# Transformer block with Strassen-type products: both bfloat16 products first in each gate/up unit, and another order for the first token pair of the down projection

## The chip, the cores and the metric

The kernel runs on one core of one Trainium2 chip. The metric is device time in microseconds, the median of several runs. The engines of the core are called PE (TensorE: matmuls and, beside them, weight loads), DVE (VectorE), ACT (ScalarE), POOL (GpSimd) and SP (SyncE, which issues nearly all DMAs here). Each engine works through its own instructions in order and waits on semaphores for the others.

## The reference

Inputs are bfloat16. `x` is 2048 tokens by 1024; the gate, up and down weights are 1024x3584, 1024x3584 and 3584x1024.

```python
mod = (silu(c) @ w_mod).reshape(1, 6, 1, -1)      # sa, ca, ga, sb, cb, gb
h = layernorm(x) * (1 + ca) + sa
x = x + ga * linear_attention(h, wqkv, wo)
h = layernorm(x) * (1 + cb) + sb
x = x + gb * ((gelu(h @ w_gate) * (h @ w_up)) @ w_down)
```

The change lies in the last line, in its gate/up products and its down projection, and in the second layernorm's modulation that feeds it.

## The kernel before, in words

**One level of Strassen-Winograd.** The gate/up products are done in 28 units, `unit(v)`, v = 0 to 27: two passes over halves of 1024 tokens (units 0 to 13 and 14 to 27), each pass over 14 slices of 256 columns of the weights. A unit computes, for gate (t = 0) and up (t = 1), a 2x2 block product with seven products instead of eight. A product is four matmuls of 128x128 weights against 512 tokens for each t, eight in all. P1 and P2 use the raw bfloat16 blocks; P3, P4, P5, P6 and P7 use sums and differences of blocks, held as float32r. The sums of the token side (`s_sum`, tiles ss, and a copy ar) are made once per pass; those of the weight side (`t_sum`, L1438, tiles tp, index k = 0, 1, 2, 4 on DVE with two instructions each, and k = 3 as two ACT copies, L1427) once per unit, ahead of it.

**Banks.** PSUM has eight banks, used as four pairs, one bank of each pair for t = 0 and one for t = 1: BA, BE, BB, BC. P1 goes to BA; ACT copies it to BB (`pcp`, L1470). P2 is accumulated onto BA, which then is one output block. P5 goes to BE and is copied to SBUF (`escp`, L1473). P6 is accumulated onto BB. DVE adds BB and the copy of P5 into BC (`padd`, L1476). P7 is accumulated onto BB, and DVE adds BB and the copy into BE (`padd` again). P3 is accumulated onto BC, P4 onto BB. Each of the four output blocks is then finished by a gelu of its gate bank (ACT, L1481) and a product with its up bank (DVE, `y_out`, L1485). The last of these, that of BB after P4, is *held*: it is issued in the next unit, between the two halves of P1. `y_store` writes two tiles per unit to DRAM.

**What sets the order.** From the gate/up units on, the order is the one in which the Python code emits instructions; no planner moves them (one does so for the attention part). PE runs the products in the order given to `unit`: 1, 5, 6, 2, 7, 3, 4; unit 0 has its own, `ORD0`, with 1, 2, 5, 6, two chunks of the attention's output projection, 7, 3, 4. P3 to P7 alternate t at each of the four steps; P1 and P2 run one t after the other. Extra work is put behind a product by `hook(v, k, fn)`: in units 1 to 8 the second layernorm of the later tokens on ACT, in units 5, 6, 9 and 10 its modulation (`mod2`, L754), in 10 to 14 the `s_sum`s (L1418) of the second pass, from 14 on the weight sums for the down projection (`b_sum`, L1577, 32 groups up to the end of unit 27). `wt_dma(v + 2)` reloads a weight slot behind P2.

**Down projection.** Eight token pairs j = 0 to 7 of 256 tokens. Its inner dimension is 14 blocks k; for k < `ns` it uses the same seven products (`dprod`, bfloat16 for 1 and 2, float32r for the others, one bank per product, banks of the pairs alternate with j), for the remaining k eight plain bfloat16 products (`plain`). `ns` is 13, but 6 for j = 0, since only six weight blocks have been summed by then; the rest (`lws`) is summed during pair 0. `y_load` fetches y into the tiles yl, `a_sum` (L1605, one ACT copy L1599) makes the token-side sums xs for the next pair, and `devac` (L1675, L1676) finishes one output quarter with two DVE instructions and a DMA. y of pair 1 overwrites that of pair 0 in the same tile.

The loop that places products and the work beside them in a unit:

Of the kernel before, what the change touches and what calls it, by code (L numbers as in the profile page):

```python
# [10 lines left out]
P = 128  # L11
# [4 lines left out]
CPG = NCH // NSG  # L16
SGW = P * CPG
NDC = D // P
# [328 lines left out]
def bass_adaLN_cond__linear_attn_block__geglu_ffn__prompt_kernel(  # L347
# [18 lines left out]
    with ExitStack() as es:  # L366
# [410 lines left out]
        def mod2(p, h, c0, n, dc0=0, dc1=NDC):  # L777
            mods(h2ap, r_h2p, (p, h), sc2, c0 * P, (c0 + n) * P, dc0, dc1, "h2")

        def mod2_act(h, c0=0, n=CPG, dc0=0, dc1=NDC):  # L780
            s0, s1 = c0 * P, (c0 + n) * P
            for dc in range(dc0, dc1):
                sA, sB, rs_ = sc2(dc)
                ap = h2ap((0, h), dc, s0, s1)
                sch.op(A, lambda e, ap=ap, sA=sA, sB=sB: e.activation(ap, ap, ACTF.Identity, bias=sB, scale=sA),
                       rd=r_h2(0, h, dc, dc + 1, s0, s1) + rs_, wr=r_h2(0, h, dc, dc + 1, s0, s1), note=f"h2modb {h}.{dc}")


        MC0 = 496
# [709 lines left out]
        def hook(v, k, fn):  # L1499
            HK.setdefault((v, k), []).append(fn)  # L1500

        def unit(v, order=(1, 5, 6, 2, 7, 3, 4)):
            more = v + 1 < 2 * NFP
            for k in order:
                if isinstance(k, tuple):
                    wo_chunk(*k)
                    continue
                if callable(k):
                    k()
                    continue  # L1510
                late = v == 0 and k == 2
                gb_, gk, yl, yh = (None, 1, 0, 0) if late else {2: (BA, 0, 0, 0), 7: (BE, 1, 1, 1), 3: (BC, 0, 1, 0), 4: (BB, 0, 0, 1)}.get(k, (None, 1, 0, 0))
                if k > 2:
                    for dc in range(ND2):
                        for t in range(2):
                            prod(v, t, k, [dc])
                for t in range(2):
                    if k < 3:
                        prod(v, t, k)
                    if k == 1:  # L1520
                        if held[0]:
                            held[0]()
                            held[0] = None
                            y_store(v - 1)
                        pcp(t)
                    elif k == 5:
                        escp(t)
                    elif k == 6:
                        padd(t, BC)
                    elif k == 7:  # L1530
                        padd(t, BE)
                    if gb_ is not None and t == gk:
                        gelu(gb_)
                        ig = (gi[0] - 1) % 2
                if k == 2 and v + 2 < 2 * NFP:
                    wt_dma(v + 2)
                if k == 4:
                    held[0] = lambda: y_out(ig, BB, v, 0, 1)
                elif gb_ is not None:
                    y_out(ig, gb_, v, yl, yh)  # L1540
                if k == 1:
                    if v == 0:
                        ar_copy(0)
                    else:
                        t_sum(v, 4)
                if more:
                    if k == (3 if v == 0 else 5):
                        t_sum(v + 1, 0)
                    if k == (3 if v == 0 else 2):
                        t_sum(v + 1, 1)  # L1550
                    if k == 3:
                        t_sum(v + 1, 3)
                        t_sum(v + 1, 2)
                for f_ in HK.pop((v, k), ()):
                    f_()

# [123 lines left out]
        def cb1():  # L1680
# [6 lines left out]
                6: lambda: (mod2(0, 0, 0, 2), x_dma(10, 12)),  # L1687
                7: lambda: (t_sum(0, 0), t_sum(0, 1), pq_scale(2, 1, GH[0] + GH[1]), x_dma(12, 14)),
                8: lambda: mod2(0, 0, 2, 2),
                9: lambda: (pq_scale(3, 0, GH[0] + GH[1]), t_sum(0, 3), mod2_act(1, 0, 2), mod2_act(1, 2, 2, ND2)),  # L1690
                10: lambda: (t_sum(0, 4), t_sum(0, 2), rb_load(3, (1,)), x_dma(14, 16), row_load(GBB, R_GBB, 2, 0, "gbb", o_gb[0]), wt_dma(1)),
                11: lambda: None,
                12: lambda: (s_sum(0, 0, 0), mod2(0, 1, 2, 2, 0, ND2)),
# [18 lines left out]
            hook(v, 3, lambda c_=c_: ln2_rows(c_))  # L1712
        for i in range(4):
            hook(i + 1, 2, lambda i=i: x1_store(i))
        for h, (v, k) in enumerate(((5, 5), (9, 4))):
            hook(v, k, lambda h=h: mod2(1, h, 0, 4, 0, ND2))
        for h, v in enumerate((6, 10)):
            hook(v, 5, lambda h=h: mod2(1, h, 0, 4, ND2, NDC))
        hook(11, 3, lambda: ar_copy(1))
        for n in range(8):  # L1720
            i, j = divmod(n, 2)
            hook(10 + (n + 1) // 2, (4, 5)[n % 2], lambda i=i, j=j: s_sum(1, i, j))
        hook(12, 2, lambda: raw_load(0))
        hook(13, 2, lambda: raw_load(1))
        ew = b_sums(range(NEA + 2))
        for n in range(4 * NEA):
            v = 14 + (n + 1) // 2
            hook(v, (4, 5)[n % 2], lambda: next(ew)())
            if n % 4 == 3 and 2 + n // 4 < NEA:
                hook(v, (4, 5)[n % 2], lambda n=n: raw_load(2 + n // 4))  # L1730
        hook(16, 2, lambda: y_load(0, 0))
        hook(17, 2, lambda: y_load(0, 1))
        hook(18, 2, lambda: raw_load(13))
        hook(24, 2, lambda: raw_load(6))
        hook(26, 2, lambda: raw_load(7))
        hook(26, 4, lambda: next(ew)())
        V_ = 2 * NFP - 1
        hook(V_, 1, lambda: next(ew)())
        hook(V_, 5, lambda: a_sum(0, 0, NEA))
        hook(V_, 5, lambda: next(ew)())  # L1740
        hook(V_, 6, lambda: (raw_load(8), a_sum(1, 0, NEA), a_sum(4, 0, NEA)))
        hook(V_, 2, lambda: (raw_load(9), raw_load(10), next(ew)(), next(ew)()))
        hook(V_, 7, lambda: (raw_load(11), raw_load(12)))
        hook(V_, 3, lambda: (next(ew)(), next(ew)()))
        hook(V_, 4, lambda: next(ew)())

# [11 lines left out]

        H = (NST + 1) // 2
        NP = S // 256  # L1760
        prev = None
        for j in range(NP):
            ns = NEA if j == 0 else NST
            lastj = j == NP - 1
            dprod(j, 1, 0, ns)
            dpcp(j)
            if j:
                devac(j - 1, 3)
                if j == 1:
                    y_load(1, 0, NEA, NKP, P, 256)  # L1770
                    y_load(1, 1, NEA, NKP, P, 256)
                    x1_load(j, 3)
                    a_sum(0, NEA, NST)
                    a_sum(1, NEA, NST)
                    a_sum(4, 0, NEA)
                    a_sum(4, NEA, NST)
                else:
                    for l in range(2):
                        y_load(j, l, NST, NKP)
                    x1_load(j, 3)  # L1780
                    a_sum(4, 0, H)
                    a_sum(4, H, NST)
            if j == 1:
                dprod(j, 5, 0, NEA)
                dprod(j, 2, 0, NEA)
                dprod(j, 5, NEA, NST)
            else:
                dprod(j, 5, 0, ns)
            descp(j)
            if j == 0:  # L1790
                a_sum(2, 0, ns)
                lws(3)
            else:
                a_sum(2, 0, H)
                a_sum(2, H, NST)
                if j < NP - 1 and j > 0:
                    y_load(j + 1, 0, 0, NST)
            dprod(j, 6, 0, ns)
            dpadd(j, BC)
            if j == 0:  # L1800
                a_sum(3, 0, ns)
            else:
                a_sum(3, 0, H)
                a_sum(3, H, NST)
            dprod(j, 2, NEA if j == 1 else 0, ns)
            plain(j, 0, 0, ns, NKP)
            if j == 0:
                y_load(1, 0, 0, NEA)
                y_load(1, 1, 0, NEA)
                lws(4)  # L1810
            elif not lastj:
                y_load(j + 1, 1, 0, NST)
            dprod(j, 7, 0, ns)
            dpadd(j, BE)
            devac(j, 0)
            if not lastj:
                for n in range(3):
                    x1_load(j + 1, n)
            if j == 0:
                a_sum(0, 0, NEA)  # L1820
                lws(4)
            elif not lastj:
                a_sum(0, 0, H)
                a_sum(0, H, NST)
            dprod(j, 3, 0, ns)
            plain(j, 0, 1, ns, NKP)
            if j == 0:
                y_load(1, 0, NEA, NKP, 0, P)
                y_load(1, 1, NEA, NKP, 0, P)
                a_sum(1, 0, NEA)  # L1830
                devac(j, 1)
                lws(4)
            else:
                devac(j, 1)
                if not lastj:
                    a_sum(1, 0, H)
                    a_sum(1, H, NST)
            plain(j, 1, 1, ns, NKP)
            if j == 0:
                lws(5)  # L1840
            devac(j, 2)
            if not lastj:
                dprod(j, 4, 0, ns)
                plain(j, 1, 0, ns, NKP)
            else:
                dprod(j, 4, 0, ns, 448)
                plain(j, 1, 0, ns, NKP, c1=448)
                plain(j, 1, 0, 0, NKP, b=BB + 1 - j % 2, c0=448, c1=512)
                devac(j, 3, 0, 448)
                devac(j, 3, 448, 512, b=BB + 1 - j % 2)  # L1850
# [76 lines left out]
```

## Time and profile before

| | |
|---|---|
| median of 3 runs | 797.11 us (795.54 to 797.56) |
| the profiled execution | 796.86 us, its span 795.0 us |
| mean granted TensorE clock | 0.995 of full speed |
| attention, up to the first product of unit 0 | 0 to 242 us |
| gate/up units | 242 to 605 us |
| down projection | 605 to 795 us |
| one gate/up unit in the middle of the second pass | 12.60 us |
| DVE busy in it, ACT busy in it | 11.19 us, 5.68 to 6.19 us |

A line of the timeline is: start in us, length in us, engine, line of the kernel, operation, output<-input tiles, shape, and xN for N instructions merged; in brackets the idle time of the engine before it, and what released it. PEld is the weight load that goes ahead of each matmul. A line of the waits is: who waited, for whom, then the total in us, how often, and the longest.

### The profile page before, as it was taken

The numbers are of one execution on the slowest core, as the hardware profiler recorded it, in microseconds if no ns is written. First come the engines' busy times: TensorE is split into PE (matmuls) and PEld (weight loads), VectorE is DVE, ScalarE is ACT, GpSimd is POOL, SyncE is SP. The second block draws the span as 40 slices with busy tenths as digits, with TensorE's granted clock in tenths as the row PEclk, the third lists the DMA queues.
The fourth block names the chain that finished last, engine by engine and source line by source line (L and its number), as shares of the span: only waits on it lengthen the run. The fifth ranks groups of instructions, "written<-read, shape, count | busy, mean of one in ns | idle before, by whom it ended". The sixth has DMA issues, their size and how long they took to land.

```text
span 795.0 us, 11012 instructions
## 1 busy us (share of the span) xinstructions
PE 778.6 (98%) x3840; PEld 497.5 (63%) x3904; DVE 637.5 (80%) x1080; ACT 341.6 (43%) x579; POOL 43.8 (6%) x126
## 2 busy tenths in 40 slices
PE   7999999999999999999999999999999989999998
PEld 4444445666445677667666777767776466666766
DVE  6799899983599887978999988888898756676664
ACT  2597743332683567575454445444454101111110
POOL 2121200000220001010000000000000000000000
PEclk9999999999999999999999999999999989999999
DMA  9789849737595477645354477545538333434340
GB/s 279 250 178 234 174 114 238 191 84 134 137 249 148 133 217 237 167 125 154 106 160 138 127 216 220 159 123 143 145 95 251 98 118 123 144 108 139 110 142 27
DMA packets 214127, 125.93 MB, mean 158 GB/s; under 512 B 74668, under 2 KB 204468, under 8 KB 214072
## 3 DMA queue, kind: packets, MB, share of 16 engines
q1 hardware_dynamic: 214056, 125.23, 58.3%
q8 instruction: 31, 0.51, 0.3%
q14 instruction: 24, 0.20, 0.1%
q10 hardware_dynamic: 16, 0.00, 0.0%
HBM read 88.35 MB, written 23.22 MB: 140 GB/s over the span
## 4 chain that ended last, share of the span: by engine, by line
PE 93%; DVE 3%; DMA 3%; issue 1%; SPq 0%; ACT 0%; DVEq 0%; ACTq 0%
PE ps_all L1464 43%; PE ps_all L1611 22%; PE ps_all L965 7%; PE ps_all L1299 7%; PE ps_all L914 6%; PE ps_all L929 6%; DMA mtb<-mb 1%; DMA wmq<-in_w_mod_dram 1%; DVE ps_all L1476 1%; DMA yl<-scr_y 1%; PE ps_all L947 0%; PE ps_all L1230 0%; PE ps_all L798 0%; DVE x1s L1676 0%; DVE ps_all L1675 0%
## 5 line engine op out<-in xcount | busy, mean ns | idle before, releaser
L1464 PE MATMUL ps_all<-ss,tp 128*128 128x512 f32 x896 | 225.9, 403 | 0.9 <-ACT ps_all L1470 0.6
L1464 PEld LDWEIGHTS ps_all<-ss,tp 128*128 128x128 f32 x896 | 167.4, 188 | 44.1 <-DVE ps_all L1476 3.5
L1611 PE MATMUL ps_all<-bt,xs 128*128 128x512 f32 (+1 forms) x485 | 122.1, 406 | 4.0 <-DVE xs L1605 4.0
L1481 ACT ACTIVATE ge<-ps_all 128x512 f32<-128x512 f32 x112 | 66.8, 596 | 134.5 <-DVE ps_all L1476 83.9
L1611 PEld LDWEIGHTS ps_all<-bt,xs 128*128 128x128 f32 x485 | 93.1, 192 | 26.3 <-DVE xs L1605 4.5
L1485 DVE TENSOR_TENSOR yr<-ge,ps_all 128x512 bf16<-128x512 f32 x112 | 76.8, 686 | 33.5 <-ACT ge L1481 15.5
L1438 DVE TENSOR_TENSOR tp<-wt 128x512 fp32r<-128x512 bf16 x112 | 72.1, 685 | 5.8 <-PE ps_all L1464 5.8
L1476 DVE TENSOR_TENSOR ps_all<-ps_all,es 128x512 f32<-128x512 f32 x112 | 72.3, 691 | 1.6 <-PE ps_all L1464 1.1
L1438 DVE TENSOR_TENSOR tp<-wt,tp 128x512 fp32r<-128x512 bf16 x112 | 72.0, 683 | 0.0
L1611 PE MATMUL ps_all<-bx,yl 128*128 128x512 bf16 (+2 forms) x269 | 57.3, 360 | 0.7
L965 PE MATMUL ps_all<-h1T,wq 128*128 128x512 bf16 x256 | 56.7, 379 | 0.0
L914 PE MATMUL ps_all<-wk,h1T 128*128 128x512 bf16 x239 | 55.3, 379 | 1.1 <-DVE h1T L754 0.6
L1299 PE MATMUL ps_all<-w,pq 128*128 128x512 bf16 x251 | 55.9, 379 | 0.4
L1464 PE MATMUL ps_all<-ar,tp 128*128 128x512 f32 x224 | 55.3, 389 | 0.0
L1644 ACT ACTIVATE ps_all<-ps_all 128x512 f32<-128x512 f32 x8 | 4.7, 582 | 116.8 <-PE ps_all L1611 116.8
L903 ACT ACTIVATE eb<-ps_all 128x512 f32<-128x512 f32 x64 | 36.4, 593 | 36.6 <-PE ps_all L914 14.8
L1464 PE MATMUL ps_all<-h21a,wt 128*128 128x512 bf16 x210 | 50.0, 380 | 1.0
L1464 PE MATMUL ps_all<-h20a,wt 128*128 128x512 bf16 x210 | 50.0, 380 | 0.9
L1464 PEld LDWEIGHTS ps_all<-ar,tp 128*128 128x128 f32 x224 | 42.0, 188 | 8.8
L1470 ACT ACTIVATE ps_all<-ps_all 128x512 f32<-128x512 f32 x56 | 32.6, 582 | 26.1 <-PE ps_all L1464 15.2
L965 PEld LDWEIGHTS ps_all<-h1T,wq 128*128 128x128 bf16 x256 | 25.0, 98 | 30.0
L1299 PEld LDWEIGHTS ps_all<-w,pq 128*128 128x128 bf16 x256 | 24.8, 98 | 30.2 <-issue 0.5
(145 smaller groups left out, 900.4 us busy)
## 6 DMA issues: line engine op xcount, KB each, us to landing
wt<-in_B_w_gate_dram SPq DMA_DIRECT2D x28, 512.0 KB, 4.1
wt<-in_B_w_up_dram SPq DMA_DIRECT2D x28, 512.0 KB, 5.0
scr_y<-yr SPq DMA_DIRECT2D x56, 256.0 KB, 2.9
yl<-scr_y SPq DMA_DIRECT2D x12, 832.0 KB, 4.3
wmst<-in_w_mod_dram SPq DMA_DIRECT2D x6, 1024.0 KB, 5.7
wmq<-in_w_mod_dram SPq DMA_DIRECT2D x8, 512.0 KB, 6.3
rb<-scr_rd SPq DMA_DIRECT2D x32, 128.0 KB, 3.0
scr_x<-xall SPq DMA_DIRECT2D x4, 1024.0 KB, 7.3
```

The lines of the kernel that those rows point to most:

```text
L903: sch.op(A, lambda e: e.activation(EB[i][:, :], PS(bank), ACTF.Exp), prd=pr(bank), wr=rng, note=f"{note}.exp")
L914: o = sch.op(T, lambda e, dc=dc: e.matmul(PS(bank), H1[sg][:, ci, dc, :], W_[:, dc, jg * 512:(jg + 1) * 512], start=(dc == 0), stop=(dc == ...
L929: o = sch.op(T, lambda e, c_=c_: e.matmul(PS(bank, 0, n), PK[c_][:, g * P:(g + 1) * P], xrow(c_, o_, o_ + n), start=(c_ == 0), stop=(c_ == ...
L965: o = sch.op(T, lambda e, dc=dc: e.matmul(PS(b), WQ[:, dc, qc * P:(qc + 1) * P], H1[sg][:, :, dc, :], start=(dc == 0), stop=(dc == NDC - 1 ...
L1299: last[half] = sch.op(T, lambda e, g=g, half=half: e.matmul(PS(b0 + half), PQ[sg][:, g, ci * P:(ci + 1) * P], W2[:, g, half * 512:(half + ...
L1438: sch.op(V, lambda e, t=t: e.tensor_tensor(TP[k][:, t, :, :], in0[:, t, :, :], in1[:, t, :, :], ALU.subtract), rd=r0[t:t + 1] + (r1[t:t + ...
L1464: o = sch.op(T, lambda e, l_=l_, r_=r_, dc=dc: e.matmul(PS(b), l_, r_, start=fresh and dc == 0, stop=dc == ND2 - 1, skip_group_check=True) ...
L1470: sch.op(A, lambda e: e.activation(PS(BB + t), PS(BA + t), ACTF.Copy), prd=pr(BA + t), pwr=pr(BB + t), note="pcp")
L1476: sch.op(V, lambda e: e.tensor_tensor(PS(dst + t), PS(BB + t), ES[t][:, :], ALU.add), prd=pr(BB + t), rd=r_2k(OFF_ES[t], f"es{t}"), pwr=pr ...
L1481: sch.op(A, lambda e: e.activation(GE[i][:, :], PS(b), ACTF.Gelu_apprx_tanh), prd=pr(b), wr=r_2k(OFF_GE[i], f"ge{i}"), note="gelu")
L1485: sch.op(V, lambda e: e.tensor_tensor(YR[:, 2 * (v % 2) + l, h * SGW:(h + 1) * SGW], GE[i][:, :], PS(b + 1), ALU.mult), rd=r_2k(OFF_GE[i], ...
L1611: pend_ = sch.op(T, lambda e, l_=l_, r_=r_, i=i: e.matmul(PS(b, c0, c1), l_, r_, start=fresh and i == 0, stop=i == n - 1, skip_group_check ...
```

## The change

In a unit, the order becomes 1, 2, 5, 6, 7, 3, 4, and P5, P6 and P7 run one t after the other, so that only P3 and P4 alternate. `t_sum(v + 1, 0)` moves from behind P5 to behind P7 (ahead of that block's output product), and `t_sum(v + 1, 1)` from behind P2 to behind P3 (also ahead of the output product). Hooks at products 4 and 5 move to 2 and 6, so do the modulation of the second pass and the `s_sum`s; part of the modulation of units 9 and 10 goes to ACT (`mod2_act` gets the pass as an argument), and all of it is done by unit 9. `ar_copy(1)` goes from unit 11 to unit 10.

In the down projection, pair 0 leaves the loop: its seven products run first, in the order 1, 5, 6, 2, 7, 3, 4, and then its plain products with k outermost. y of pair 1 is loaded in a first part (k < 6) behind P2 and in five slices behind k = 7, 9, 11, 12 and 13. The weight sums and the sums for pair 1 are spread over these. The four output quarters of pair 0 are finished during pair 1, whose P5 is no longer split.

```diff
-        def unit(v, order=(1, 5, 6, 2, 7, 3, 4)):
+        def unit(v, order=(1, 2, 5, 6, 7, 3, 4)):
...
-                if k > 2:
+                if k in (3, 4):
                     for dc in range(ND2):
                         for t in range(2):
                             prod(v, t, k, [dc])
                 for t in range(2):
-                    if k < 3:
+                    if k not in (3, 4):
                         prod(v, t, k)
...
+                if more and k == (3 if v == 0 else 7):
+                    t_sum(v + 1, 0)
+                if more and k == 3:
+                    t_sum(v + 1, 1)
                 if k == 4:
                     held[0] = lambda: y_out(ig, BB, v, 0, 1)
                 elif gb_ is not None:
...
-                if more:
-                    if k == (3 if v == 0 else 5):
-                        t_sum(v + 1, 0)
-                    if k == (3 if v == 0 else 2):
-                        t_sum(v + 1, 1)
-                    if k == 3:
-                        t_sum(v + 1, 3)
-                        t_sum(v + 1, 2)
+                if more and k == 3:
+                    t_sum(v + 1, 3)
+                    t_sum(v + 1, 2)
...
-        for h, (v, k) in enumerate(((5, 5), (9, 4))):
-            hook(v, k, lambda h=h: mod2(1, h, 0, 4, 0, ND2))
-        for h, v in enumerate((6, 10)):
-            hook(v, 5, lambda h=h: mod2(1, h, 0, 4, ND2, NDC))
-        hook(11, 3, lambda: ar_copy(1))
+        for n in range(4):
+            hook(5 + n // 2, (2, 6)[n % 2], lambda n=n: mod2(1, 0, 0, 4, 2 * n, 2 * n + 2))
+        hook(9, 6, lambda: mod2(1, 1, 0, 4, 0, 3))
+        hook(9, 4, lambda: mod2(1, 1, 0, 4, 3, 5))
+        hook(9, 6, lambda: mod2_act(1, 1, 0, 4, 5, 6))
+        hook(9, 3, lambda: mod2_act(1, 1, 0, 4, 6, 8))
+        hook(10, 3, lambda: ar_copy(1))
         for n in range(8):
             i, j = divmod(n, 2)
-            hook(10 + (n + 1) // 2, (4, 5)[n % 2], lambda i=i, j=j: s_sum(1, i, j))
+            hook(10 + n // 2, (2, 6)[n % 2], lambda i=i, j=j: s_sum(1, i, j))
...
         for n in range(4 * NEA):
-            v = 14 + (n + 1) // 2
-            hook(v, (4, 5)[n % 2], lambda: next(ew)())
+            v, k = 14 + n // 2, (2, 6)[n % 2]
+            hook(v, k, lambda: next(ew)())
...
+        hook(26, 6, lambda: next(ew)())
         hook(26, 4, lambda: next(ew)())
...
+        dprod(0, 1, 0, NEA)
+        dpcp(0)
+        dprod(0, 5, 0, NEA)
+        descp(0)
+        a_sum(2, 0, NEA)
+        lws(3)
+        dprod(0, 6, 0, NEA)
+        dpadd(0, BC)
+        a_sum(3, 0, NEA)
+        dprod(0, 2, 0, NEA)
+        for l in range(2):
+            y_load(1, l, 0, NEA)
+        dprod(0, 7, 0, NEA)
+        dpadd(0, BE)
+        dprod(0, 3, 0, NEA)
+        dprod(0, 4, 0, NEA)
+        lws(6)
+        for k in range(NEA, NKP):
+            for s_ in range(2):
+                for c in range(2):
+                    plain(0, s_, c, k, k + 1)
+            for k0, k1 in {7: ((6, 8),), 9: ((8, 10),), 11: ((10, 12),), 12: ((12, 13),), 13: ((13, 14),)}.get(k, ()):
+                for l in range(2):
+                    y_load(1, l, k0, k1)
...
+        for j in range(1, NP):
             lastj = j == NP - 1
-            dprod(j, 1, 0, ns)
+            dprod(j, 1, 0, NST)
             dpcp(j)
-            if j:
+            if j == 1:
+                a_sum(4, 0, NEA)
+                a_sum(4, NEA, NST)
+                devac(0, 0)
+                devac(0, 1)
+            else:
                 devac(j - 1, 3)
...
-            if j == 1:
-                dprod(j, 5, 0, NEA)
-                dprod(j, 2, 0, NEA)
-                dprod(j, 5, NEA, NST)
```

More of the change, by code (lines that the diff above doesn't have):

```diff
@@ L778, in mod2, with mod2_act @@
             mods(h2ap, r_h2p, (p, h), sc2, c0 * P, (c0 + n) * P, dc0, dc1, "h2")
-        def mod2_act(h, c0=0, n=CPG, dc0=0, dc1=NDC):
+        def mod2_act(p, h, c0=0, n=CPG, dc0=0, dc1=NDC):
             s0, s1 = c0 * P, (c0 + n) * P
@@ L783, in mod2_act @@
                 sA, sB, rs_ = sc2(dc)
-                ap = h2ap((0, h), dc, s0, s1)
+                ap = h2ap((p, h), dc, s0, s1)
                 sch.op(A, lambda e, ap=ap, sA=sA, sB=sB: e.activation(ap, ap, ACTF.Identity, bias=sB, scale=sA),
-                       rd=r_h2(0, h, dc, dc + 1, s0, s1) + rs_, wr=r_h2(0, h, dc, dc + 1, s0, s1), note=f"h2modb {h}.{dc}")
+                       rd=r_h2(p, h, dc, dc + 1, s0, s1) + rs_, wr=r_h2(p, h, dc, dc + 1, s0, s1), note=f"h2modb {h}.{dc}")
         MC0 = 496
@@ L1689, in bass_adaLN_cond__linear_attn_block__geglu_ffn__prompt_kernel @@
                 8: lambda: mod2(0, 0, 2, 2),
-                9: lambda: (pq_scale(3, 0, GH[0] + GH[1]), t_sum(0, 3), mod2_act(1, 0, 2), mod2_act(1, 2, 2, ND2)),
+                9: lambda: (pq_scale(3, 0, GH[0] + GH[1]), t_sum(0, 3), mod2_act(0, 1, 0, 2), mod2_act(0, 1, 2, 2, ND2)),
                 10: lambda: (t_sum(0, 4), t_sum(0, 2), rb_load(3, (1,)), x_dma(14, 16), row_load(GBB, R_GBB, 2, 0, "gbb", o_gb[0]), wt_dma(1)),
@@ L1726, in bass_adaLN_cond__linear_attn_block__geglu_ffn__prompt_kernel @@
         for n in range(4 * NEA):
-            v = 14 + (n + 1) // 2
-            hook(v, (4, 5)[n % 2], lambda: next(ew)())
+            v, k = 14 + n // 2, (2, 6)[n % 2]
+            hook(v, k, lambda: next(ew)())
             if n % 4 == 3 and 2 + n // 4 < NEA:
-                hook(v, (4, 5)[n % 2], lambda n=n: raw_load(2 + n // 4))
+                hook(v, k, lambda n=n: raw_load(2 + n // 4))
         hook(16, 2, lambda: y_load(0, 0))
@@ L1735, in bass_adaLN_cond__linear_attn_block__geglu_ffn__prompt_kernel @@
         hook(26, 2, lambda: raw_load(7))
+        hook(26, 6, lambda: next(ew)())
         hook(26, 4, lambda: next(ew)())
         V_ = 2 * NFP - 1
-        hook(V_, 1, lambda: next(ew)())
+        hook(V_, 2, lambda: (raw_load(9), raw_load(10), next(ew)()))
         hook(V_, 5, lambda: a_sum(0, 0, NEA))
-        hook(V_, 5, lambda: next(ew)())
         hook(V_, 6, lambda: (raw_load(8), a_sum(1, 0, NEA), a_sum(4, 0, NEA)))
-        hook(V_, 2, lambda: (raw_load(9), raw_load(10), next(ew)(), next(ew)()))
-        hook(V_, 7, lambda: (raw_load(11), raw_load(12)))
+        hook(V_, 7, lambda: (raw_load(11), raw_load(12), next(ew)(), next(ew)()))
         hook(V_, 3, lambda: (next(ew)(), next(ew)()))
@@ L1760, in bass_adaLN_cond__linear_attn_block__geglu_ffn__prompt_kernel, with halves @@
         NP = S // 256
-        prev = None
-        for j in range(NP):
-            ns = NEA if j == 0 else NST
+        def halves(i):
+            a_sum(i, 0, H)
+            a_sum(i, H, NST)
+        dprod(0, 1, 0, NEA)
[11 more added lines that the diff above has]
+        dprod(0, 7, 0, NEA)
@@ new lines, in bass_adaLN_cond__linear_attn_block__geglu_ffn__prompt_kernel @@
+        dpadd(0, BE)
[9 more added lines that the diff above has]
+                    y_load(1, l, k0, k1)
+            if k == 7:
+                a_sum(0, 0, NEA)
+                a_sum(1, 0, NEA)
+            elif k == 9:
+                lws(4)
+            elif k == 11:
+                lws(4)
+                a_sum(0, NEA, 8)
@@ L1764, in bass_adaLN_cond__linear_attn_block__geglu_ffn__prompt_kernel @@
+        lws(3)
+        a_sum(0, 8, NST)
+        a_sum(1, NEA, NST)
+        for n in range(3):
+            x1_load(1, n)
+        for j in range(1, NP):
             lastj = j == NP - 1
-            dprod(j, 1, 0, ns)
+            dprod(j, 1, 0, NST)
             dpcp(j)
-            if j:
-                devac(j - 1, 3)
-                if j == 1:
[L1770 to L1782, printed above, removed]
@@ L1783, in bass_adaLN_cond__linear_attn_block__geglu_ffn__prompt_kernel @@
-            if j == 1:
-                dprod(j, 5, 0, NEA)
-                dprod(j, 2, 0, NEA)
-                dprod(j, 5, NEA, NST)
[L1787 to L1798, printed above, removed]
@@ L1799, in bass_adaLN_cond__linear_attn_block__geglu_ffn__prompt_kernel @@
-            dpadd(j, BC)
[L1800 to L1811, printed above, removed]
+            if j == 1:
[4 more added lines that the diff above has]
+            else:
+                devac(j - 1, 3)
+                for l in range(2):
+                    y_load(j, l, NST, NKP)
+                a_sum(4, 0, H)
+                a_sum(4, H, NST)
@@ L1812, in bass_adaLN_cond__linear_attn_block__geglu_ffn__prompt_kernel @@
+            x1_load(j, 3)
+            dprod(j, 5, 0, NST)
+            descp(j)
+            halves(2)
+            if not lastj:
+                y_load(j + 1, 0, 0, NST)
+            if j == 1:
+                devac(0, 2)
+            dprod(j, 6, 0, NST)
+            dpadd(j, BC)
+            halves(3)
+            if j == 1:
+                devac(0, 3)
+            dprod(j, 2, 0, NST)
+            plain(j, 0, 0, NST, NKP)
+            if not lastj:
                 y_load(j + 1, 1, 0, NST)
-            dprod(j, 7, 0, ns)
+            dprod(j, 7, 0, NST)
@@ L1818, in bass_adaLN_cond__linear_attn_block__geglu_ffn__prompt_kernel @@
                     x1_load(j + 1, n)
[L1819 to L1840, printed above, removed]
+                halves(0)
+            dprod(j, 3, 0, NST)
+            plain(j, 0, 1, NST, NKP)
+            devac(j, 1)
+            if not lastj:
+                halves(1)
+            plain(j, 1, 1, NST, NKP)
             devac(j, 2)
             if not lastj:
-                dprod(j, 4, 0, ns)
-                plain(j, 1, 0, ns, NKP)
-            else:
-                dprod(j, 4, 0, ns, 448)
-                plain(j, 1, 0, ns, NKP, c1=448)
+                dprod(j, 4, 0, NST)
+                plain(j, 1, 0, NST, NKP)
+            else:
+                dprod(j, 4, 0, NST, 448)
+                plain(j, 1, 0, NST, NKP, c1=448)
                 plain(j, 1, 0, 0, NKP, b=BB + 1 - j % 2, c0=448, c1=512)
```

## The prediction

> **What bounds the kernel now.** I read the page first, then the waits of TensorE (PE), then busy time by stage, then the order of instructions across one gate/up unit, and last the places where PE stands still. The page and PE's waits, longest first, say that little is left to win on PE:
>
> ```profile
> PE 778.6 (98%) x3840; PEld 497.5 (63%) x3904; DVE 637.5 (80%) x1080; ACT 341.6 (43%) x579; POOL 43.8 (6%) x126
> ...
> PE ps_all L1611 <- DVE xs L1605: 4.0, 1, 4.0
> PE ps_all L657 <- POOL bmask L610: 2.1, 1, 2.1
> PE ps_all L798 <- DMA wmq<-in_w_mod_dram: 1.6, 1, 1.6
> ```
>
> Only the 4.0 us wait lies in code that changes. Busy time by stage (columns: window, length, busy PE, weight load, VectorE, ScalarE, GpSimd with counts, granted clock, DMA share, GB/s) shows one gate/up unit, then the stretch around that wait and the one behind it:
>
> ```profile
> 507.87:520.47 12.60, 12.53 (x57) 8.92 (x57) 11.19 (x18) 6.19 (x11) 0.00 (x0) 1.00 0.59 167
> ...
> 620.00:638.30 18.30, 14.28 (x65) 7.14 (x64) 12.76 (x20) 3.54 (x5) 0.00 (x0) 0.98 0.41 100
> 638.30:653.80 15.50, 15.48 (x55) 11.51 (x57) 8.27 (x10) 0.60 (x1) 0.00 (x0) 0.81 0.35 111
> ```
>
> A unit takes 12.60 us. Its floor: 16 bf16 matmuls at 0.2158 (64 of L965 take 13.83 us on the chain of waits) and 40 float32r at 0.2267 (the eight of P4 start at 502.62, the next unit at 504.44) are 12.52; 0.08 is left for two switches from float32r to bf16 and back. So a unit is PE-bound, and VectorE, at 11.19 of 12.60, is second. What matters is not its sum but its order. The timeline across a unit's end:
>
> ```profile
> 501.08 1.29 DVE L1476 TENSOR_TENSOR ps_all<-ps_all,es 128x512 f32<-128x512 f32 x2
> ...
> 502.46 1.51 DVE L1485 TENSOR_TENSOR yr<-ge,ps_all 128x512 bf16<-128x512 f32 x2
> ...
> 503.89 1.28 DVE L1438 TENSOR_TENSOR tp<-wt 128x512 fp32r<-128x512 bf16 x2
> ...
> 504.44 1.90 PE L1464 MATMUL ps_all<-h21a,wt 128*128 128x512 bf16 x8
> 504.49 0.60 ACT L1481 ACTIVATE ge<-ps_all 128x512 f32<-128x512 f32 x1 [0.20 <-PE ps_all L1464]
> 505.09 0.68 DVE L1577 TENSOR_TENSOR bt<-wst 128x512 fp32r<-128x512 bf16 x1
> 505.51 0.58 ACT L1470 ACTIVATE ps_all<-ps_all 128x512 f32<-128x512 f32 x1 [0.43 <-PE ps_all L1464]
> 505.69 0.68 DVE L1485 TENSOR_TENSOR yr<-ge,ps_all 128x512 bf16<-128x512 f32 x1
> 505.99 2.19 PE L1464 MATMUL ps_all<-ss,tp 128*128 128x512 f32 x8
> ...
> 506.47 0.58 ACT L1470 ACTIVATE ps_all<-ps_all 128x512 f32<-128x512 f32 x1 [0.37 <-DVE yr L1485]
> ```
>
> Call T the start of P1 (504.44). The previous unit's last output product (505.69, L1485) reads bank BB+1, so the second copy of P1 (506.47, L1470), which overwrites BB+1, waits for it. It ends at T+2.61, and nobody cares, because P5 comes next on PE and touches neither bank.
>
> **The change, part by part.**
>
> *Order P1, P2 in every unit.* P2 accumulates onto banks BA that the copies read, so P2's half t now waits for copy t. Unit 0 has this order already, with ScalarE free and no held product:
>
> ```profile
> 243.43 0.58 ACT L1470 ACTIVATE ps_all<-ps_all 128x512 f32<-128x512 f32 x1 [5.48 <-PE ps_all L1464]
> 244.06 0.56 PEld L1464 LDWEIGHTS ps_all<-h20a,wt 128*128 128x128 bf16 x4 [0.30 <-ACT ps_all L1470]
> 244.29 0.58 ACT L1470 ACTIVATE ps_all<-ps_all 128x512 f32<-128x512 f32 x1 [0.28 <-PE ps_all L1464]
> 244.93 0.56 PEld L1464 LDWEIGHTS ps_all<-h20a,wt 128*128 128x128 bf16 x4 [0.30 <-ACT ps_all L1470]
> ```
>
> Its 16 bf16 matmuls still start 0.216 apart, so the copies just fit: cost zero, margin zero. Hence any delay of the second copy goes straight to PE, and behind that wait stand P2's second half, P5, P6, P7.
>
> *VectorE's queue in front of the held product.* Now, after the second P7 sum (L1476; start 501.69), come two outputs, one tsum pair, one bsum, then the held product: T+1.25. After the change tsum0 and tsum1 of the next unit stand there too: sum, tsum0 (2), output, tsum1 (2), output, tsum2 (2), held product. All inputs are ready (each gelu ends earlier), so the queue runs at its pace: a tsum pair 1.21 (495.46 to 496.67), an output 0.60, the sum 0.60: nine instructions, 5.44. P3 and P4 are 16×0.2267=3.63 long, P7's last matmul starts 0.227 before them and lasts 0.389, so P7 ends at T-3.47 in either order; the sum starts 0.04 later, at T-3.43. The held product starts at T+2.01, ends +2.69; copy +0.10 (as 506.37 to 506.47) and 0.58: T+3.37; weight load and matmul 0.09 later (unit 0): P2's second half starts at T+3.46 instead of T+12×0.2158=2.59. **0.87 us per unit**, renewed each unit since VectorE waits for P6 and P7 again afterwards. Bounds: 0 (the copies hide, as in unit 0) to 1.3 (1.29 is what unit 1 loses today to the same wait: its P6 comes at 266.57, about 265.4 was due). I take 0.87, from the rows of this very stretch.
>
> Boundary by boundary: units 1 to 8 have layernorm work on ScalarE (sq 1.14, xhat 1.13) before the last gelu; that puts the first copy at T+1.66 to 2.24, P2's first half 0.6 late, still inside 0.87: 8×0.87=6.96. Unit 9: three mod2 (pace 0.32) in front of the P7 sums, two behind, 1.73. Unit 10: ar_copy (1.96) in front of gelu, 1.44. Units 11 to 13: an ssum (1.13) after the P6 sums delays the P7 sums by 0.39: 3×1.26=3.78. Units 14 to 25: the bsum at P6 fits in a pause: 12×0.87=10.44. Unit 26: a bsum in front of the held product, 1.48. Unit 1 loses 1.43 where it loses 1.29 now: +0.14. Sum **+26.0**.
>
> *P7 straight behind P6.* P7 accumulates onto BB, which the P6 sum reads; P2 stood between them. P5, P6, P7 now run half by half, so the first sum starts 0.43 after P6's first half issues its last matmul, takes 0.69 (L1476 median 690 ns), hop 0.05, while the second half covers 1.13. A late float32r weight load cost 0.11 at 410.18 (that matmul lasted 0.50, others 0.39). 0.43+0.69+0.05+0.11-1.13 = 0.14, times 27 = **+3.8** (bounds 0 and 0.25, the latter with a whole 0.19 weight load exposed and some hop). The half-by-half order itself costs nothing: float32r in the down projection runs that way at the same 0.227.
>
> *One switch less per unit:* half of 0.08, times 27: **-1.1**. *Moved hooks:* units 1 to 27 take 329.8 us (268.47 to 598.26) for 26 periods, 2.2 over 26×12.60, lost where mod2 and ssum delay the P6 sums, as at 410; those pieces now lie elsewhere and are priced above: **-2.2**. Six more SP issues (0.4 to 0.5 each) for the smaller reloads, and later wt loads, are covered by an SP queue that is mostly idle; uncovered they would cost 3.
>
> *First token pair.* Today its second neighbour loads y only after pair 0's plain products, and PE waits 3.97 us at 634.3 for a load that landed at 637.0. The clock then falls: 0.81 over the next stretch, 55 matmuls in 15.52 instead of 12.57, another 2.95. In the new order y comes in six slices behind each k; the last needed 64 KB slice (landing 2.0) goes out 1.7 us before pair 1 starts and is used 2.6 after its start. VectorE's four output products move out of pair 0 into pair 1, which has room. **-6.9** (bounds 0 and 6.9). [...] But P7 of pair 0 now follows P2 at once: the P6 sum stands behind one asum and three bsums (610.94 to 611.63), P7 was due at 610.84: **+0.95**.
>
> Sum: 26.0+3.8-1.1-2.2-6.9+0.95 = +20.5. The profiled execution took 796.86 us (span 795.0), 0.25 below the median 797.11. 796.9+20.5 = **817.4**.
>
> **Rivals.**
> Faster: the held product doesn't bind. If VectorE reached it by T+1.14, the copies would fit as in unit 0, and P7's wait might vanish too; left are -1.1-2.2-6.9+0.95: 787.6. For it: 80% VectorE load and unit 0's rows. Against it: nine instructions at 0.60 do not fit into the 4.57 us from T-3.43 to T+1.14; two would have to go. 9%.
> Half: the stall exists but is under 0.5 us (a faster pace, or P3 and P4 held up as well): about 800 to 806. 7%.
> Slower still: the pauses, about 1 us in each 13.6, drop the clock. 26 times 2.95 more, 894. Against it: unit 1's 1.29 us pause left the clock at 1.00. [...] 3%.
> More stalls: something unpriced in pair 1 or the late wt loads, 826 to 840. 8%.
>
> **How the numbers follow.** My forecast has 73%. Its own range: (a) at three quarters and no P7 wait gives 807; P7 at 0.25, half the clock loss kept and 0.1 more per unit gives 826. With the rivals outside holding about 2 in 10, the range is 806 to 826. Faster by over 0.3% (about what a measurement can tell) only in the first rival: 0.09; within it 0.02; slower 0.89.
>
> **What would show it.** Units about 13.57 us long, in 14 to 25 above all; weight loads of P2 waiting for the ScalarE copy of L1470 and that copy for the product of L1485, some 0.9 us per unit; a short wait of P7 for the sum. The down projection without the 4.0 us wait and with clock 1.00 there. Wrong if units stay at 12.6, or if P2 waits but VectorE stands idle before the held product.

## The result and the profile after

The changed kernel takes 820.7 us (median of 4 runs, 819.64 to 821.61), the kernel before, beside it, 797.34 us: a ratio of 1.030, with a 95% interval of 1.028 to 1.032. It is slower by 23 us. The profiled execution took 819.64 us with a span of 817.8; before it was 796.86 with 795.0.

The page's first lines and the waits of PE and of its weight loads (PEld), after:

```profile
PE 786.7 (96%) x3840; PEld 491.3 (60%) x3904; DVE 636.1 (78%) x1078; ACT 346.0 (42%) x582; POOL 46.2 (6%) x126
...
PE ps_all L1464 <- ACT ps_all L1470: 19.0, 36, 1.2
...
PE ps_all L1610 <- DVE ps_all L1651: 0.9, 1, 0.9
...
PEld ps_all L1464 <- ACT ps_all L1470: 42.6, 56, 1.7
PEld ps_all L1464 <- DVE ps_all L1476: 10.4, 28, 0.4
```

Busy VectorE time is nearly the same (636.1 against 637.5 us) and the number of matmuls too. What is new is PE waiting for the ScalarE copy of P1 (L1470), which it did for 0.6 us before, and weight loads waiting for the sum of P6 (L1476) in every unit, 28 of them against 11 before. The 4.0 us wait for y is gone; 0.9 us of waiting for the sum in pair 0 (L1651) stands in its place. The two totals of the weight loads also hold a pause between one load and the next that PE does not see (0.30 us each in unit 0), so here the count says more than the sum.

Where the 22.8 us of span come from, by the first weight load of each part: the gate/up units took 363.1 us (242.16 to 605.23) and take 391.5 (242.50 to 634.01), +28.4. The down projection took 189.77 and takes 183.83, -5.9. The unchanged attention in front differs by 0.34.

A unit in the middle of the second pass and the two stretches of the down projection that answer to those shown before (columns as before; the first window is one unit long):

```profile
538.22:551.87 13.65, 12.95 (x55) 8.73 (x56) 11.18 (x20) 6.21 (x12) 0.00 (x0) 1.00 0.55 155
634.02:657.00 22.98, 21.96 (x98) 12.16 (x100) 19.28 (x30) 5.11 (x9) 0.00 (x0) 1.00 0.45 132
657.00:680.00 23.00, 22.90 (x102) 15.74 (x103) 17.36 (x23) 2.77 (x4) 0.00 (x0) 1.00 0.51 157
```

The unit is 13.65 us long instead of 12.60, and the clock stays at 1.00 where pair 1 starts (0.81 before). The timeline of this unit's sums of P6 and of its end shows both new waits:

```profile
545.30 0.70 DVE L1476 TENSOR_TENSOR ps_all<-ps_all,es 128x512 f32<-128x512 f32 x1 [1.45 <-PE ps_all L1464]
...
546.05 3.52 PEld L1464 LDWEIGHTS ps_all<-ss,tp 128*128 128x128 f32 x16 [0.38 <-DVE ps_all L1476]
...
547.40 1.52 DVE L1476 TENSOR_TENSOR ps_all<-ps_all,es 128x512 f32<-128x512 f32 x2
548.82 1.28 DVE L1438 TENSOR_TENSOR tp<-wt 128x512 fp32r<-128x512 bf16 x2
...
550.03 0.68 DVE L1485 TENSOR_TENSOR yr<-ge,ps_all 128x512 bf16<-128x512 f32 x1
550.62 1.28 DVE L1438 TENSOR_TENSOR tp<-wt,tp 128x512 fp32r<-128x512 bf16 x2
551.83 0.68 DVE L1485 TENSOR_TENSOR yr<-ge,ps_all 128x512 bf16<-128x512 f32 x1
552.43 1.28 DVE L1438 TENSOR_TENSOR tp<-wt 128x512 fp32r<-128x512 bf16 x2
552.72 0.58 ACT L1470 ACTIVATE ps_all<-ps_all 128x512 f32<-128x512 f32 x1 [0.43 <-PE ps_all L1464]
553.63 0.68 DVE L1485 TENSOR_TENSOR yr<-ge,ps_all 128x512 bf16<-128x512 f32 x1
554.40 0.58 ACT L1470 ACTIVATE ps_all<-ps_all 128x512 f32<-128x512 f32 x1 [1.10 <-DVE yr L1485]
555.03 0.55 PEld L1464 LDWEIGHTS ps_all<-h21a,wt 128*128 128x128 bf16 x4 [1.12 <-ACT ps_all L1470]
555.04 1.04 PE L1464 MATMUL ps_all<-h21a,wt 128*128 128x512 bf16 x4 [0.63 <-ACT ps_all L1470]
```

Read it from below. P2's second half starts at 555.04, behind the second copy (554.40), which waits for the held product (553.63), in front of which nine VectorE instructions run without a pause from the second P7 sum on. The unit starts at 551.65 (the first copy begins 1.06 behind a unit's start), so the half was due at 554.24: 0.80 late. Above, the weight load of P7 (546.05) comes 0.05 after the first P6 sum (545.30) has ended. Its matmul was due at 545.94 and is in effect at 546.16 (the next one starts at 546.39, one matmul of 0.23 later): 0.23 late.

### The profile page after: what moved, and what is told of

Read it like the earlier page. It is cut to its first block, busy times and chain, and to the rows that moved or that the text cites. A ratio compares the mean times of both kernels' runs of the same rounds, so it can differ in the third digit from the quotient of the medians.

```text
span 817.8 us, 10975 instructions
## 1 busy us (share of the span) xinstructions
PE 786.7 (96%) x3840; PEld 491.3 (60%) x3904; DVE 636.1 (78%) x1078; ACT 346.0 (42%) x582; POOL 46.2 (6%) x126
## 5 line engine op out<-in xcount | busy, mean ns | idle before, releaser
L1464 PE MATMUL ps_all<-ss,tp 128*128 128x512 f32 x896 | 221.7, 401 | 0.0
L1464 PEld LDWEIGHTS ps_all<-ss,tp 128*128 128x128 f32 x896 | 165.1, 188 | 48.1 <-DVE ps_all L1476 10.4
L1610 PE MATMUL ps_all<-bt,xs 128*128 128x512 f32 (+1 forms) x485 | 118.5, 399 | 0.9 <-DVE ps_all L1651 0.9
L1476 DVE TENSOR_TENSOR ps_all<-ps_all,es 128x512 f32<-128x512 f32 x112 | 77.3, 697 | 51.1 <-PE ps_all L1464 49.4
L1610 PEld LDWEIGHTS ps_all<-bt,xs 128*128 128x128 f32 x485 | 91.1, 188 | 22.3 <-DVE ps_all L1651 1.4
L1464 PE MATMUL ps_all<-h20a,wt 128*128 128x512 bf16 x211 | 51.8, 380 | 10.2 <-ACT ps_all L1470 9.3
L1610 PE MATMUL ps_all<-bx,yl 128*128 128x512 bf16 (+1 forms) x267 | 59.7, 360 | 0.8
L1473 ACT ACTIVATE es<-ps_all 128x512 f32<-128x512 f32 x56 | 33.5, 598 | 50.4 <-PE ps_all L1464 50.4
L1470 ACT ACTIVATE ps_all<-ps_all 128x512 f32<-128x512 f32 x56 | 32.6, 582 | 40.2 <-DVE yr L1485 22.8
L1464 PEld LDWEIGHTS ps_all<-h20a,wt 128*128 128x128 bf16 x224 | 18.7, 98 | 42.0 <-ACT ps_all L1470 21.8
```

What stands on the lines that cost most here:

```text
L1464: o = sch.op(T, lambda e, l_=l_, r_=r_, dc=dc: e.matmul(PS(b), l_, r_, start=fresh and dc == 0, stop=dc == ND2 - 1, skip_group_check=True) ...
L1470: sch.op(A, lambda e: e.activation(PS(BB + t), PS(BA + t), ACTF.Copy), prd=pr(BA + t), pwr=pr(BB + t), note="pcp")
L1473: sch.op(A, lambda e: e.activation(ES[t][:, :], PS(BE + t), ACTF.Copy), prd=pr(BE + t), wr=r_2k(OFF_ES[t], f"es{t}"), note="escp")
L1476: sch.op(V, lambda e: e.tensor_tensor(PS(dst + t), PS(BB + t), ES[t][:, :], ALU.add), prd=pr(BB + t), rd=r_2k(OFF_ES[t], f"es{t}"), pwr=pr ...
L1610: pend_ = sch.op(T, lambda e, l_=l_, r_=r_, i=i: e.matmul(PS(b, c0, c1), l_, r_, start=fresh and i == 0, stop=i == n - 1, skip_group_check ...
```

## The experiments

The theory is that two waits between neighbours on PE cost the units 28 us: P2's for the copy, because of the queue in front of the held product, and P7's for the sum of P6. The rivals were that P2 cannot stand behind P1 at all, that the moved sums cost something in any order, and that the two parts of the change influence each other.

**The parts apart.** Two kernels: the units of before with the new token pair, and the new units with the down projection of before.

```diff
  # pair_only: before.py, with everything from "H = (NST + 1) // 2" to the end of the down projection from the changed kernel
  # units_only: the changed kernel, with that stretch from before.py
```

> The gate/up units as before, only the first token pair and its neighbour as changed. If the two parts add up, the down projection takes 183.8 us as in the changed kernel instead of 189.8, the 4.0 us wait for y and the low clock behind it are gone, a wait of about 0.9 us for the sum of P6 comes in, and the time is 797.3-6.0 = 791.3 us (790 to 793). Rival: pair 0 gains only because the units before it leave more time for loads, then the time stays at 795 or above.

> The gate/up units as changed, the down projection as before. Theory: the units cost 28.4 us by themselves, and the wait for y and the low clock are back: 797.3+28.4 = 825.7 us (824 to 828). Rival: the late loads at the end of the changed units shift what the down projection does, then the down projection is not 189.8 us long.

Measured: the pair alone 791.84 us, 0.9942 of the kernel before (0.9927 to 0.9957); the units alone 825.1, 1.0354 (1.0337 to 1.0371). Their down projections last 183.9 and 189.7 us by the trace. In the first the clock stays at 1.00; in the second the wait for y and the low clock are back:

```profile
PE ps_all L1611 <- DVE ps_all L1652: 0.9, 1, 0.9
...
625.00:640.00 15.00, 15.00 (x69) 8.78 (x69) 11.17 (x17) 3.40 (x5) 0.00 (x0) 1.00 0.35 105
```

```profile
PE ps_all L1610 <- DVE xs L1604: 3.9, 1, 3.9
...
667.00:683.00 16.00, 15.95 (x59) 11.75 (x60) 8.78 (x11) 0.60 (x1) 0.00 (x0) 0.82 0.36 116
```

(The first fence is of the pair alone, the second of the units alone; each has a line of PE's waits and one window.) The parts add up: +28.4 and -4.9 by the medians against +23.4 together. The pair's 4.9 is less than the 5.9 that its down projection gained in the profiled execution; there the attention, which is unchanged, ended 2.2 us later than before, for a reason that is not shown. The rival of the first run (no gain without the new units) is out, and so is that of the second: its down projection is as long as before.

**The order of products alone.** The changed kernel with the old order:

```diff
-        def unit(v, order=(1, 2, 5, 6, 7, 3, 4)):
+        def unit(v, order=(1, 5, 6, 2, 7, 3, 4)):
...
-            hook(10 + n // 2, (2, 6)[n % 2], lambda i=i, j=j: s_sum(1, i, j))
+            hook(10 + n // 2, (6, 2)[n % 2], lambda i=i, j=j: s_sum(1, i, j))
```

(Likewise for the other two pairs of hooks.)

> The changed kernel with its products in the order 1, 5, 6, 2, 7, 3, 4 again (the hooks at 2 and 6 change places so that they keep their own order); the sums stay in front of the held product, and P5, P6, P7 stay half by half. Theory: the queue on VectorE is as long as in the changed kernel, the second copy still ends at T+3.3, but P6's second half needs it only at T+4.4, and P2 lies between P6 and P7 again, so both waits go: units of 12.60, 820.7-28.4-3.0 = about 789 us (787 to 792). Rival: the sums in front of the held product cost PE time in any order, then units stay above 13 us and the time above 810.

Measured: 788.74 us, 0.990 of the kernel before (0.9885 to 0.9914). All units from 1 to 27 are 12.60 us long, those that had cost more before included; a window as long as one unit (columns as before):

```profile
489.68:502.28 12.60, 12.53 (x57) 8.93 (x57) 11.08 (x19) 6.10 (x12) 0.00 (x0) 1.00 0.60 171
```

The sums of the next unit stand in front of the held product as in the changed kernel, and PE no longer waits for VectorE in any unit. So the moved sums cost nothing by themselves; the order of P1, P2 and of P6, P7 turns them into a wait. The new hooks and the half-by-half order, taken together with the old order, are an improvement (which of the two brings it was not separated): unit 1 fell from 13.44 to 12.60, units 5, 6, 10 and 12 lost their extra 0.4 to 0.6 us.

**Only one neighbourhood.** P5 between P1 and P2, P7 still straight behind P6:

```diff
-        def unit(v, order=(1, 2, 5, 6, 7, 3, 4)):
+        def unit(v, order=(1, 5, 2, 6, 7, 3, 4)):
```

> The changed kernel with the order 1, 5, 2, 6, 7, 3, 4: P5 covers the copies, P7 still comes straight behind P6. Theory: only the held product's wait goes, the wait of P7 for the sum (0.23 us per unit) stays, units of about 12.88 us, 820.7-22.5 = 798 us (796 to 801). Rival: most of the loss is the wait of P7, then the time stays above 812.

Measured: 803.49 us, 1.0081 of the kernel before (1.0066 to 1.0096), 5 more than expected and outside the expected range. Units without hooks at 2 and 6 are about 12.8 us long, close to the 12.88 expected; but those with a weight sum there are 13.15, and those with an ssum 13.7. The timeline of one of them:

```profile
505.58 0.69 DVE L1485 TENSOR_TENSOR yr<-ge,ps_all 128x512 bf16<-128x512 f32 x1 [1.75 <-PE ps_all L1464]
506.19 0.68 DVE L1576 TENSOR_TENSOR bt<-wst 128x512 fp32r<-128x512 bf16 x1
506.79 1.29 DVE L1476 TENSOR_TENSOR ps_all<-ps_all,es 128x512 f32<-128x512 f32 x2
507.54 3.50 PEld L1464 LDWEIGHTS ps_all<-ss,tp 128*128 128x128 f32 x16 [0.68 <-DVE ps_all L1476]
```

P2 now stands directly ahead of P6, so its output and the piece hooked behind it run while P6's first half runs, and the sum starts that much later, with P7 waiting. The rival (most of the loss is P7's wait) is out: the time fell by 17 us. The expectation had overlooked a third neighbour, which the changed kernel does not have because P5 lies between P2 and P6 there.

**The queue alone, shorter and longer.** The order of products stays as changed. First, tsum2, which only P7 needs, goes behind the held product; second, tsum4 goes ahead of it.

```diff
  # tsum2_behind
                     t_sum(v + 1, 3)
-                    t_sum(v + 1, 2)
+                    if v == 0:
+                        t_sum(v + 1, 2)
...
                         t_sum(v, 4)
+                        if v > 1:
+                            t_sum(v, 2)
```

```diff
  # tsum4_ahead
                     if k == 1:
+                        if t == 0 and v > 0:
+                            t_sum(v, 4)
                         if held[0]:
                             held[0]()
...
-                    else:
-                        t_sum(v, 4)
```

> The changed kernel, its order of products kept, but from unit 2 on the pair of tsum2 (needed only by P7) is issued in the unit itself, behind the held product and tsum4. That takes two of nine instructions, 1.21 us, from the queue in front of the held product. Theory: the 0.79 us wait of P2 goes in the units without layernorm work (15 to 26: about 12.87 us, what stays is the 0.23 us of P7), shrinks by 1.2 in units 10 and 12 to 14, and stays mostly in units 2 to 9 and 11, where ScalarE brings the first copy late: 820.7-16.4 = about 804 us (800 to 808). Rival: P2 straight behind P1 can't be covered in a full unit whatever stands on VectorE; then units stay at 13.6 and the time at 818 to 821.

> The changed kernel with two instructions more in front of the held product: the pair of tsum4, which stood behind it, goes ahead of it. Theory: each unit from 1 on gets 1.21 us longer, 14.85 in the middle of the second pass, less where ScalarE was the later one: 820.7+26x1.2 = about 851 us (846 to 854). Rival: the wait is set by ScalarE or by the bank, then nothing changes.

Measured: 802.19 us (1.0068 of the kernel before, 1.0051 to 1.0084) and 860.46 us (1.0798, 1.0776 to 1.0819). The middle units are 12.83 and 14.85 us long, against 13.65: two instructions less take 0.8, which is all of this wait in the middle units, two more add the full 1.2. With the shorter queue the second copy starts as soon as P1's second half is done, and P2 starts on time:

```profile
527.61 0.58 ACT L1470 ACTIVATE ps_all<-ps_all 128x512 f32<-128x512 f32 x1 [0.43 <-PE ps_all L1464]
528.24 0.56 PEld L1464 LDWEIGHTS ps_all<-h21a,wt 128*128 128x128 bf16 x4 [0.30 <-ACT ps_all L1470]
528.47 0.58 ACT L1470 ACTIVATE ps_all<-ps_all 128x512 f32<-128x512 f32 x1 [0.28 <-PE ps_all L1464]
529.10 0.56 PEld L1464 LDWEIGHTS ps_all<-h21a,wt 128*128 128x128 bf16 x4 [0.30 <-ACT ps_all L1470]
```

From the second line on, the idle times in the brackets are those of unit 0 of the kernel before. So P2 can stand behind P1 in a full unit, and the rival is out. Units 2 to 9, with layernorm on ScalarE ahead of the copies, go from about 13.6 to 13.3 only: in unit 4 the first copy starts at 304.98, 1.57 behind the unit's start instead of 1.06. There 0.47 of the 0.8 us stays although the queue is shorter (13.30 against 12.83), so the queue is the whole cause only in the units without layernorm. The longer queue's time lies outside the expected 846 to 854 us; most of the excess is the clock (last section).

**The halves.** The changed kernel with P5, P6 and P7 alternating the halves again:

```diff
-                if k in (3, 4):
+                if k > 2:
...
-                    if k not in (3, 4):
+                    if k < 3:
```

> The changed kernel, but P5, P6 and P7 alternate the halves again. Theory: both halves of P6 now end together, so the two sums of P6 stand between P6 and P7 in full (wait about 1.25 us instead of 0.23), and the sums of P7 start 0.45 later, which the held product passes on: about 1.45 us more per unit, 859 us (845 to 862). Rival: the order of the halves costs nothing, then 821.

Measured: 857.05 us, 1.0755 of the kernel before (1.0733 to 1.0776); middle units 15.05 us long, 1.40 more than with halves in a row. In the unit that starts at 565.21, P7's matmuls are 1.28 late instead of 0.23 (the third starts at 575.25, due 573.97), and P2's second half 1.17 instead of 0.80 (568.97, due 567.80): both terms of the expectation are there, 1.25 and 0.45 by its reckoning. So the half-by-half order is worth 36 us once P7 stands behind P6; the wait of P7 is real and moves as the sums of P6 do.

**Pair 0, and the fastest version.** On top of the old order, the sum of P6 ahead of the weight sums in pair 0:

```diff
-        lws(3)
         dprod(0, 6, 0, NEA)
         dpadd(0, BC)
+        lws(1)
         a_sum(3, 0, NEA)
+        lws(2)
```

> The fastest version so far (old order of products in the units, all else as changed), and in pair 0 the sum of P6 stands ahead of the three weight sums instead of behind them. Theory: the 0.90 us wait of P7 in pair 0 goes: 788.7-0.9 = 787.8 us (787 to 789), no wait of PE for DVE in the down projection. Rival: the weight sums come too late for pair 1 instead, then the time stays at 788.7 or above.

Measured: 787.82 us, 0.9884 of the kernel before (0.9869 to 0.9899). The wait of 0.9 us is gone from PE's waits; none for VectorE or y is left in the units or in the down projection. The whole list of PE's waits, except one of 0.2 us in the attention:

```profile
PE ps_all L657 <- POOL bmask L610: 2.1, 1, 2.1
PE ps_all L947 <- DMA mtb<-mb: 0.7, 1, 0.7
PE ps_all L798 <- DMA wmq<-in_w_mod_dram: 0.5, 2, 0.3
PE ps_all L914 <- DVE h1T L754: 0.2, 1, 0.2
```

This is 33 us faster than the changed kernel and 9 us faster than the one before. Its step beyond the old order, 788.74 to 787.82, is of the size of the wait, but about as small as these measurements can tell; the trace settles it, with a down projection of 183.0 us instead of 183.8.

## Why the prediction was right, point by point

- **The direction and the place.** 817.4 us were forecast, 820.7 measured, inside 806 to 826. Of the 3.3 us between them 1.9 lie in the units and 0.3 in the attention, and 1.1 is the median's distance from the profiled execution. (The upper end's terms, with half of the 2.95 us of low clock, add up to 824.5, not 826.) The step that decided, the queue of nine VectorE instructions in front of the held product, is in the trace as it was worked out: held product at T+1.98 (forecast 2.01), second copy at T+2.75 (2.79), P2's second half at T+3.39 (3.46). The shorter and the longer queue show that it is the cause, in full in the units without layernorm and in part in units 2 to 9.
- **Its size.** All units from 1 on together: the sum of their lengths above 12.83 (what tsum2_behind leaves in units without this wait) is 25.2 us. The forecast's terms, with the whole 1.43 of unit 1, make 27.3. Per middle unit it is 0.80 instead of 0.87, since the held product came 0.03 earlier and the copy with its hops took 0.04 less. The special cases came out close: unit 10 14.46 us (its forecast 12.60+1.73+0.10), unit 11 14.09 (14.14), units 12 and 14 13.97 (13.96), unit 27 14.20 (14.18). Unit 13 was longer, 14.19 (13.96): its second copy starts 0.37 after the held product has ended instead of 0.09 (431.04 to 431.41), and what it waited for is not shown.
- **P7 behind P6.** Right in kind, too small: 0.23 us per unit instead of 0.14, 6.2 us in all instead of 3.8, just inside its bound of 0.25. (Its terms as written add up to 0.15.) The term that was off is the time from P6's last matmul to the start of the sum: 0.11 us (545.19 to 545.30) where 0.04 had been taken from a wait in the down projection.
- **One switch less.** Forecast -1.1, measured about zero: with the held product's wait gone and one switch left, a unit takes 12.83 = 12.52+0.23+0.08, and 0.08 is what two switches left over before. (The two rows named for the 12.52 give 0.2161 and 0.2275 per matmul; starts of single matmuls give the 0.2158 and 0.2267 that were used.) The trace shows where the saving went. Behind a switch to float32r the first matmuls start up to 0.236 apart instead of 0.2267, and behind the pause of P7 they do so again: the six from 546.39 to 547.79 take 1.40 us where 1.36 was due, about the 0.04 that the missing switch had saved.
- **Moved hooks.** The 2.2 us of the mod2 and ssum units are indeed gone in the old order. Of unit 1's loss, 1.29 had been counted as there before; its length, 13.44 against 12.60, says 0.84. (PE stood idle for 0.59 us there, so this was no pause of 1.29 us, and it said less about the clock than the prediction took from it.) These four, -2.1 (size), +2.4 (P7), +1.1 (switch) and +0.45 (unit 1), are the 1.9 us by which the units' forecast, 26.5, fell short of 28.4. They partly cancel, and in this the closeness of the total is luck.
- **The token pair.** Forecast -6.9+0.95 = -5.95, measured -5.9 in the down projection; both the clock and the 0.90 us of the sum came as worked out. The pauses in the changed kernel's units, at most 1.23 us, left the clock at 1.00; in tsum4_ahead pauses of 2.41 and 2.18 us came with half clock (last section).
- **The rivals.** The faster one needed the queue to be two instructions shorter; tsum2_behind is that case, and the wait vanished as stated there in the middle units. Its price of 787.6 was not reached (802.19), since P7's wait stayed and layernorm on ScalarE still held up P2 in units 2 to 9. The rival "Half" is out, with 0.80 us per middle unit, and so is "More stalls", with the down projection as long as forecast. The clock rival did not come true at these pauses (at most 1.23 us, clock 1.00).

## What to carry to other kernels

The busy share of an engine does not say whether a piece of work on it is free; what counted here is how many instructions stand in its queue between the last moment at which they may start and the next result for which the bounding engine waits. When products that share an accumulator become neighbours, count copy, sum and everything queued in front of them against the length of half a product; here two instructions too many cost 0.8 us in each middle unit and about 0.3 in those where ScalarE was late anyway. A rearrangement of such a kernel should be split into its parts: of this one, the token pair was good by itself, and the order of products alone turned 8 us of gain into 23 us of loss.

## What the runs showed of the hardware that was not expected

Pauses on PE shorter than that of the kernel before came with a lower clock too. There, the wait of 3.97 us (634.29 to 638.26) came with 6.83 us at half clock (637.44 to 644.27). In tsum4_ahead the trace has four stretches of 3.41 us at half clock, in units 10, 13, 14 and 27; PE paused for 2.41 us in unit 13 and for 2.18 us in unit 14. Another pause of 2.40 us, which the two windows from 263.56 to 270.39 share (0.99 and 1.40 us of idle time), left the clock at 1.00, and so did the 1.82 us of idle time in the window from 585. Windows of that run: the first of the four stretches, one around the second, one in the quiet part, and the two with the pause of 2.40 us (length, then busy PE; granted clock is the third number from the end):

```profile
403.50:406.92 3.42, 3.42 (x10) 2.45 (x8) 1.82 (x2) 0.56 (x2) 0.00 (x0) 0.50 0.93 244
447.00:462.00 15.00, 12.59 (x49) 9.07 (x48) 10.11 (x16) 4.32 (x9) 0.00 (x0) 0.89 0.50 140
585.00:600.00 15.00, 13.18 (x59) 8.79 (x58) 11.35 (x20) 5.70 (x10) 0.00 (x0) 1.00 0.39 105
263.56:266.97 3.41, 2.42 (x12) 0.81 (x9) 3.41 (x7) 0.88 (x2) 0.00 (x0) 1.00 0.00 0
266.97:270.39 3.42, 2.02 (x9) 1.44 (x10) 1.35 (x3) 1.10 (x3) 0.00 (x0) 1.00 0.40 110
```

Units 10, 13, 14 and 27 are 2.8 us longer than in the changed kernel, and the longer queue accounts for 1.2 of it. So each stretch cost about 1.6 us, together 6.5 of the 9.5 us by which that run exceeded its expectation. Another 1.2 is that 27 units got longer, not the 26 that were counted.

The length of a pause does not sort the cases: 2.18 us came with half clock and 2.40 us did not. What does is not shown. The pauses are read from the ends of matmuls, which are modelled.
